# Two queues for the first loads, and the second layer's sums on VectorE

## The chip, the cores and the metric

One NeuronCore of one Trainium2 chip. The metric is the device time of one execution, in microseconds; of several executions the median is taken.

## What is computed

Three stages follow each other. The float64 inputs of the two layers' weights are read as pairs of words and turned into float32 on the chip.

```
# attention: 4 x 8 heads, 576 positions, 64 wide; window 128, slope per head
scores = where(mask, q @ k.T / 8 - slope * distance, -1e9)
attn   = softmax(scores);  x = attn @ v          # x: 2304 x 512
# layer 1: 512 -> 2048 -> 512, rational function
h = x @ w_in;  g = (a0 + a1 h + a2 h^2 + a3 h^3) / (1 + |b0||h| + |b1| h^2 + 1e-6)
x = g @ w_out
# layer 2: 512 -> 2048 -> 512, ELU
h = x @ w2_in; g = where(h > 0, h, exp(min(h, 0)) - 1)
out = g @ w2_out
```

## The kernel before

**Order of the work.** The program is written for manual scheduling: every engine runs its instructions in the order in which the Python code emits them, and an instruction at the head of an engine's queue that waits holds up all behind it. Tiles are named after the buffers in which they lie, so that `q_wi` is a tile of q in a slot that later holds a piece of `w_in`.

**Attention** runs over 16 units (a pair of heads of one batch element). `load(u, what)` (L336 to 356) brings q, k or v of a unit into SBUF by three DMAs, two of 128 KB and a tail of 32 KB, all issued by `nc.sync`, SP's queue (L348, L352). Ahead of the loop the loads of units 0 and 1 are issued in the order q0, k0, q1, k1, v0, v1 (L634 to 638). Those of unit u+2 are issued where unit u has been transposed. The hand-written list STEPS gives, for each turn t of the loop, the order of some 65 steps and the unit (t plus an offset) on which each works: `qT` and `kT` are TensorE's transposes of q and k (L418), with offsets 3 and 2, `qC` and `kC` their copies out of PSUM by ScalarE and VectorE (L441, L443), `zT` the tails' transposes (L432), S0 to S4 the score matmuls (L456, L474) and D0 to D8 VectorE's additions of the bias with a running extreme (L500). The transpose of q of unit 2 therefore stands in TensorE's order ahead of score matmuls of unit 1. Before all this, ScalarE's table of functions is loaded (L1255), and TensorE does warm-up matmuls on zeros (L646).

**Layer 1** goes over 6 blocks of 384 tokens and 16 pieces of 128 hidden features. Every product is made of three float32r passes (high x high, low x high, high x low): a value is split into a rounded high part, copied by ScalarE, and the rest, subtracted by VectorE or GpSimd.

**Layer 2** multiplies blocks by a scheme with seven products in place of eight. It goes over 3 blocks J of 768 tokens and 8 pairs p of hidden pieces, 24 steps q. A step has seven first products (`product`, L918) called b11, b21, t2, t3, t1, t4, b22, and four second ones (`gemm2`, L934). The factors t1 to t4 and s1 to s4 are sums:

- `sum_w(q)` (L837 to 848) makes the four sums of weights of a step, four operations of 128x256, into two tiles s; they are also written to DRAM (`keep_sums`) and read back for the later blocks (`load_sums`). So they are made for steps 0 to 7 alone.
- `sum_x(J, n)` (L881 to 896) makes one of the four sums of activations of a block, two operations of 128x384, in place of the block before it (which is used up by then) in xT.

Sums, and every other operand, are then split by `hi_w` (L870) or `hi_op` (L905) on ScalarE and `lo` (L875) on VectorE. A first product lies in one of two PSUM banks until VectorE has added it to what it belongs to (`added`, L974); ELU follows with two ScalarE operations (L980, L984), one on VectorE (L989) and the split of the result (L1006, L875).

The order of layer 2 is made by a planner, `in_order`: `step(key, engine, cost, fn, *needs)` notes each piece of work with a cost in ns, and what it needs. A due time is worked out backwards from the users. Then, always for the engine that can begin first, the ready step with the earliest start is taken, and of those within 60 ns the one with the earliest due time. A step on SP counts as done 3500 ns after its cost, any other 200 ns after. TensorE's own order is fixed. Products cost 1040 ns (first) and 2080 ns (second).

The lines that matter here: of the weight sums (L1051), step 0 is made ahead of the plan by VectorE (AT_DVE), w = 1 is planned on VectorE at 1400 ns, and w = 2 to 7 on GpSimd at 3500 ns. They need the load of the step's weights (`load_wi`, L810), the splits of step w-1's sums, since they use the same two tiles, and its `kept`. The activation sums (L1084) of block 0 are made by VectorE ahead of the plan, and those of blocks 1 and 2 are planned on GpSimd at 2300 ns each, sum n after product b11 of step 3+n, or 11+n, and after the splits of block J-1.

Of the kernel before, what the change touches and what calls it, by code (L numbers as in the profile page):

```python
# [44 lines left out]
def kernel(  # L45
# [13 lines left out]
    nc = tc.nc  # L59
# [40 lines left out]
    def place(key, shape, dtype, what):  # L100
        nm = "_".join(map(str, SLOT[key]))
        return wpool.tile(shape, dtype, tag=nm, name=f"{what}_{nm}")
# [107 lines left out]
    def cv_tile(shape, dtype, name, n=None):  # L210
        n = next(n_cv) if n is None else n
        return cv.tile(shape, dtype, tag=f"cv{n}", name=f"{name}{n}")
# [112 lines left out]
    def attention():  # L325
        with ExitStack() as es:
# [11 lines left out]
            def load(u, what):  # L338
                b, p = units[u]
                for nm in what:  # L340
                    src = {"q": q, "k": k, "v": v}[nm]
                    shape = [P, NF + 1, 2, D]
                    if nm == "v":
                        t = vt[u % 2]
                    else:
                        t = place(LATE["qk".index(nm) * 2 + u % 2], shape, F32, nm)
                    for e in range(2):
                        nc.sync.dma_start(  # L348
                            out=t[:, 0:NF, e, :],
                            in_=src[b, 2 * p + e, 0:NF * P, :].rearrange("(t p) d -> p t d", p=P),  # L350
                        )
                    nc.sync.dma_start(  # L352
                        out=t[0:TL, NF, :, :],
                        in_=src[b, 2 * p:2 * p + 2, NF * P:S, :].rearrange("h p d -> p h d"),
                    )
                    raw_t[nm, u] = t
# [254 lines left out]
            def run(step, u):  # L611
# [7 lines left out]
                elif 0 <= u < NU:  # L619
# [8 lines left out]
                    elif step == "Y":  # L628
                        if u + 2 < NU:
                            load(u + 2, "v")  # L630
                        else:
                            load_some(2)

            load(0, "q")  # L634
            load(0, "k")
            load(1, "qk")
            load(0, "v")
            load(1, "v")

            zero = place(order[19], [P, 4 * P], F32, "zero")  # L640
            nc.vector.memset(zero, 0.0)
# [51 lines left out]
    def experts():  # L693
# [47 lines left out]
        OPS, XO, sums, G, sq, kept, low_part = {}, {}, {}, {}, {}, {}, {}  # L741
# [65 lines left out]
        def load_wi(q):  # L807
            two[q] = t = at(q, "C", [P, 2, PC], F32, "two")
            for e in range(2):
                nc.sync.dma_start(out=t[:, e], in_=joined["wi", KF + q % NP2 * 2 + e])  # L810
# [26 lines left out]
        def sum_w(q, eng=nc.gpsimd, ns=range(4)):  # L837
            w = two[q]
            a11, a12, a21, a22 = [w[:, e, h * HC:(h + 1) * HC] for e in range(2) for h in range(2)]
            if 0 in ns:  # L840
                sq[q] = [cv_tile([P, 2, HC], F32, "s", n) for n in range(2)]
            s = sq[q]
            for n in ns:
                x, y, op = (
                    (a21, a22, ALU.add), (s[0][:, 0], a11, ALU.subtract), (a11, a21, ALU.subtract),
                    (a12, s[0][:, 1], ALU.subtract),
                )[n]
                eng.tensor_tensor(out=s[n // 2][:, n % 2], in0=x, in1=y, op=op)

        def keep_sums(w):  # L850
            kept[w] = [dram.tile([P, PC], F32, name=f"sums_{w}_{n}") for n in range(2)]
            for d, t in zip(kept[w], sq[w]):
                nc.sync.dma_start(out=d, in_=t.rearrange("p s c -> p (s c)"))
# [6 lines left out]
        def hi_w(q, x):  # L860
            if x in "CD":
                src = sq[q]["CD".index(x)].rearrange("p s c -> p (s c)")
            elif x == "B":
                src = two[q][:, 1, HC:PC]
            elif x == "A":
                src = two[q][:, 0]
            else:
                src = pair[0][:, "EF".index(x)]
            OPS[q, x] = t = at(q, x, [P, 2, HC if x == "B" else PC], F32R, "op")
            nc.scalar.activation(out=t[:, 0], in_=src, func=AF.Copy)  # L870
            low_part[q, x] = (t[:, 1], src, t[:, 0])

        def lo(key, eng=nc.vector):
            out, src, hi = low_part.pop(key)
            eng.tensor_tensor(out=out, in0=src, in1=hi.bitcast(F32), op=ALU.subtract)  # L875

        def x_row(J, k, T):
            c0 = (2 * J + T) * TB
            return xT[:, k, c0:c0 + TB]

        def sum_x(J, n, eng=nc.gpsimd, ks=range(2)):  # L881

            if 0 not in ks:
                pass
            elif J == 0:
                nm = "_".join(map(str, t_slots[n]))
                t = wpool.tile([P, 2, TB], F32, tag=nm, name=f"t_{nm}")
                sums[J, n] = [t[:, k] for k in range(2)]
            else:
                sums[J, n] = [x_row(J - 1, k + 2 * (n // 2), n % 2) for k in range(2)]  # L890
            for k in ks:
                b11, b21, b12, b22 = [x_row(J, k + 2 * i, T) for T in range(2) for i in range(2)]
                x, y = (
                    (b12, b11), (b22, sums[J, 0][k]), (b22, b12), (b21, sums[J, min(n, 1)][k]),
                )[n]
                eng.tensor_tensor(out=sums[J, n][k], in0=x, in1=y, op=ALU.subtract)
# [63 lines left out]
        def step(key, engine, cost, fn, *needs):  # L960
            todo[key] = (engine, cost, fn, needs)
            if engine == "PE":
                pe_order.append(key)
# [71 lines left out]
        def weight_steps(w):  # L1035

            def part(x, cost_hi, cost_lo, *needs):
                step((w, "hi", x), "ACT", cost_hi, lambda: hi_w(w, x), *needs)
                step((w, "lo", x), "DVE", cost_lo, lambda: lo((w, x)), (w, "hi", x))

            if w == 0:
                step((w, "kept"), "SP", 1200, lambda: keep_sums(w))
            else:
                out_gone = [(w - 2, "out", T, t) for T in range(2) for t in range(NTT)]
                if w > 1:
                    step((w, "load"), "SP", 1200, lambda: load_wi(w), (w - 3, "t1"), (w - 3, "t2"))
                gone = [(w - 1, "lo", "C"), (w - 1, "lo", "D")]
                if w >= NP2:
                    step((w, "sum"), "SP", 1200, lambda: load_sums(w), *gone)
                else:  # L1050
                    eng, cost, at = (nc.vector, 1400, "DVE") if w == 1 else (nc.gpsimd, 3500, "POOL")  # L1051
                    step((w, "sum"), at, cost, lambda: sum_w(w, eng), (w, "load"), *gone, (w - 1, "kept"))
                    step((w, "kept"), "SP", 1200, lambda: keep_sums(w), (w, "sum"))
                part("A", 520, 600, (w, "load"), (w - 3, "b11"), (w - 3, "b21"), *out_gone)
                part("B", 300, 340, (w, "load"), (w - 3, "t4"), *out_gone)
                part("C", 520, 600, (w, "sum"), (w, "lo", "A"), (w, "lo", "B"))
                part("D", 520, 600, (w, "sum"), (w - 3, "t3"), (w - 3, "b22"), *out_gone)
            for e, x in enumerate("EF"):
                gone = [(w - 2, "G", n) for n in ((0, 3), (1, 2))[e]]
                if e in raw_ones(w):  # L1060
                    if w > 0:
                        step((w, "raw", x), "SP", 600, lambda e=e: load_raw(w, e), *gone)
                    step((w, "scale", x), "ACT", 570, lambda e=e: scale_wo(w, e), (w, "raw", x), (w - 1, "lo", x),
                         (w - 1, "keep", x))
                    step((w, "words", x), "DVE", 1600, lambda e=e: join_wo(w, e), (w, "scale", x))
                    step((w, "keep", x), "SP", 600, lambda e=e: keep_wo(w, e), (w, "words", x))
                else:
                    step((w, "words", x), "SP", 600, lambda e=e: load_wo(w, e), (w - 1, "lo", x),
                         (w - 1, "keep", x), (w - NP2, "keep", x))
                part(x, 520, 600, (w, "words", x), *gone)  # L1070
# [9 lines left out]
        def x_sums(J, q):  # L1080

            used = [("xlo", J - 1, nm, k) for nm in ORDER for k in range(2)]
            for n in range(4):
                step(("sum", J, n), "POOL", 2300, lambda n=n: sum_x(J, n), *used, (q - 4 + n, "b11"),  # L1084
                     *[("sum", J, i) for i in range(n)])

        def second(q):
# [164 lines left out]
        last_pair()  # L1252

    with tc.manual_schedule():
        nc.scalar.preload_act_table_set("natural_log_exp_and_others")  # L1255
        attention()
        experts()

# [29 lines left out]
```

## Time and profile before

| | |
|---|---|
| median of 3 runs | 953.41 us (953.21 to 955.58) |
| profiled execution | 951.87 us, of which the span of the trace is 950.2 |
| TensorE, VectorE, ScalarE busy | 97%, 86%, 78% |
| GpSimd busy | 26% |
| chain that ended last | TensorE 63%, VectorE 18%, ScalarE 14%, issue 4%, DMA 1% |
| stages | attention to about 160 us, layer 1 to about 560, layer 2 to the end |

Busy times count an engine's instructions; for TensorE matmuls are pipelined, so what tells is the time in which it does nothing. A timeline row gives the start, the duration, engine, line, operation and tiles (out<-in) and, in brackets, how long the engine had been idle before it and what ended that. PEclk is the granted clock of TensorE as a share of its full 2.4 GHz. SPq is the issuing of DMAs by SP.

### The profile page before, as it was taken

Reading aid. Unit: us, or ns where it says so; the run is one execution under the profiler, and the core shown is the slowest. Engines: PE = TensorE matmul, PEld = TensorE weight load, DVE = VectorE, ACT = ScalarE, POOL = GpSimd, SP = SyncE. Lnnn points to the kernel's source line nnn. Section 1 sums busy time; section 2 is a strip of 40 time slices with the busy share of each in tenths; the row PEclk is TensorE's granted clock in tenths of the full one; section 3 lists DMA queues with packets and bytes.
Section 4 is the critical chain, followed back from the end, with each engine's and each line's share of the span. In section 5 each row is a group of like instructions: output and inputs, shape, how many; then the busy total and the mean of one; then the engine's idle time right before and its main releaser. Section 6 shows DMA issues by size and latency. Waiting matters only on the chain.

```text
span 950.2 us, 16856 instructions
## 1 busy us (share of the span) xinstructions
PE 920.9 (97%) x5494; PEld 839.0 (88%) x5494; DVE 818.8 (86%) x1890; ACT 745.1 (78%) x1635; POOL 248.6 (26%) x312
## 2 busy tenths in 40 slices
PE   7999998999999999999999999999999999999998
PEld 5766767999999999999999988878889898989897
DVE  5999998999999999999999999899987678787653
ACT  4999999889889889889888986656777566766553
POOL 4777772122222222222222225350310000000000
PEclk8999999999999999999999999999999999999999
DMA  6899943011231222222210034434344332443201
GB/s 165 207 236 242 235 135 95 1 34 34 84 100 51 84 83 68 84 67 86 82 46 28 26 120 125 142 122 152 104 140 149 100 100 68 162 141 96 78 1 67
DMA packets 112424, 98.36 MB, mean 104 GB/s; under 512 B 62800, under 2 KB 86096, under 8 KB 112336
## 3 DMA queue, kind: packets, MB, share of 16 engines
q1 hardware_dynamic: 112336, 97.29, 35.1%
q8 instruction: 43, 0.70, 0.3%
q14 instruction: 45, 0.37, 0.1%
HBM read 79.96 MB, written 17.30 MB: 102 GB/s over the span
## 4 chain that ended last, share of the span: by engine, by line
PE 63%; DVE 18%; ACT 14%; issue 4%; DMA 1%; POOL 0%; SPq 0%; DVEq 0%; ACTq 0%; POOLq 0%
PE acc L934 17%; PE h L260 15%; PE acc L705 15%; PE m L918 14%; ACT pT L441 2%; ACT pr_wo L515 2%; ACT pr_wi L515 2%; DVE ghi L301 2%; DVE qq L304 1%; DVE ee L322 1%; DVE ee L318 1%; DVE qq L313 1%; DVE h L321 1%; DVE op_wi L875 1%; DVE op_wo L875 1%
## 5 line engine op out<-in xcount | busy, mean ns | idle before, releaser
L260 PE MATMUL h<-xs,w_wi 128*128 128x384 f32 x1152 | 218.1, 335 | 1.3 <-ACT xs L235 0.8
L260 PEld LDWEIGHTS h<-xs,w_wi 128*128 128x128 f32 x1152 | 200.4, 188 | 4.2 <-DVE xs L236 2.4
L705 PE MATMUL acc<-ghi,w_wo 128*128 128x384 f32 x768 | 195.0, 334 | 0.0
L319 POOL TENSOR_TENSOR glo<-ee,rr 128x384 fp32r<-128x384 f32 x92 | 93.5, 1016 | 315.8 <-DVE ee L318 160.9
L705 PEld LDWEIGHTS acc<-ghi,w_wo 128*128 128x128 f32 x768 | 138.7, 188 | 0.0
L705 PE MATMUL acc<-glo,w_wo 128*128 128x384 f32 x384 | 128.7, 335 | 0.9 <-DVE glo L319 0.5
L934 PE MATMUL acc<-op_wo,ghi 128*128 128x512 f32 x288 | 89.6, 392 | 0.0
L307 ACT ACTIVATE rr<-qq,c_q 128x384 f32<-128x384 f32 x96 | 59.3, 618 | 38.5 <-DVE qq L304 37.7
L918 PE MATMUL m<-xo_wo,op_wi 128*128 128x384 f32 x336 | 77.1, 337 | 7.2 <-DVE ee L974 4.0
L918 PE MATMUL m<-xo_wi,op_wi 128*128 128x384 f32 x336 | 77.2, 337 | 0.0
L980 ACT ACTIVATE oo<-qq 128x384 f32<-128x384 f32 x24 | 12.6, 525 | 79.0 <-DVE qq L974 79.0
L705 PEld LDWEIGHTS acc<-glo,w_wo 128*128 128x128 f32 x384 | 72.1, 188 | 2.0 <-POOL glo L319 1.2
L918 PEld LDWEIGHTS m<-xo_wo,op_wi 128*128 128x128 f32 x336 | 60.4, 188 | 13.0 <-DVE qq L974 3.7
L290 ACT ACTIVATE oo<-h,a_sb 128x384 f32<-128x384 f32 x96 | 67.8, 706 | 4.6 <-DVE h L321 3.7
L293 ACT ACTIVATE ee<-h,a_sb 128x384 f32<-128x384 f32 x96 | 67.5, 703 | 0.0
L301 DVE TENSOR_TENSOR ghi<-ee,rr 128x384 fp32r<-128x384 f32 x96 | 53.6, 558 | 12.2 <-ACT oo L290 0.5
L322 DVE TENSOR_TENSOR ee<-ee,h 128x384 f32<-128x384 f32 x96 | 53.2, 555 | 10.0
L934 PEld LDWEIGHTS acc<-op_wo,ghi 128*128 128x128 f32 x288 | 53.5, 188 | 8.9
L918 PEld LDWEIGHTS m<-xo_wi,op_wi 128*128 128x128 f32 x336 | 60.5, 188 | 0.0
L304 DVE SCALAR_TENSOR_TENSOR qq<-h,b_abs,qa 128x384 f32<-128x384 f32 x92 | 55.9, 608 | 3.7 <-ACT qa L289 3.7
L974 DVE TENSOR_TENSOR ee<-ee,m 128x384 f32<-128x384 f32 x96 | 52.5, 547 | 5.2 <-PE m L918 5.1
L934 PE MATMUL acc<-op_wo,glo 128*128 128x512 f32 x144 | 57.0, 396 | 0.0
(203 smaller groups left out, 2175.1 us busy)
## 6 DMA issues: line engine op xcount, KB each, us to landing
pair<-joined_wo SPq DMA_DIRECT2D x43, 256.0 KB, 2.7
raw_wo<-in_moe_w_out_dram SPq DMA_DIRECT2D x20, 512.0 KB, 5.1
raw_wi<-in_moe_w_in_dram SPq DMA_DIRECT2D x16, 512.0 KB, 4.6
half<-in_moe_w_in_dram SPq DMA_DIRECT2D x32, 256.0 KB, 2.7
two_wo<-joined_wi SPq DMA_DIRECT2D x32, 256.0 KB, 2.9
s<-sums SPq DMA_DIRECT2D x32, 256.0 KB, 2.8
half<-in_moe_w_out_dram SPq DMA_DIRECT2D x22, 256.0 KB, 2.8
v<-in_v_dram SPq DMA_DIRECT2D x32, 128.0 KB, 3.2
```

Of the source, the lines that this page charges most:

```text
L260: nc.tensor.matmul(h, lhsT=WT["wi", f][:, SEL[wp], kk * P:(kk + 1) * P], rhs=x[xp][kk], start=(kk == 0 and n == 0), stop=(kk == KD - 1 and ...
L290: nc.scalar.activation(out=oo, in_=h2, func=AF.Identity, scale=a_sb[:, 3:4], bias=a_sb[:, 1:2])
L293: nc.scalar.activation(out=ee, in_=h2, func=AF.Identity, scale=a_sb[:, 2:3], bias=a_sb[:, 0:1])
L301: nc.vector.tensor_tensor(out=hi, in0=ee0, in1=rr0, op=ALU.mult)
L304: nc.vector.scalar_tensor_tensor(out=qq, in0=h2, scalar=b_abs[:, 1:2], in1=qa, op0=ALU.mult, op1=ALU.add)
L307: nc.scalar.activation(out=rr, in_=qq, func=AF.Ln, bias=c_q)
L319: (nc.gpsimd if c > 4 else nc.vector).tensor_tensor(out=low, in0=ee0, in1=rr0, op=ALU.mult)
L322: nc.vector.tensor_tensor(out=ee, in0=ee, in1=h, op=ALU.add)
L705: nc.tensor.matmul(acc_t[d], lhsT=WT["wo", f][:, SEL[wp], d * P:(d + 1) * P], rhs=gt[SEL[xp]], start=(f == 0 and n == 0), stop=(f == KF - ...
L918: nc.tensor.matmul(out, lhsT=w[:, SEL[wp], c0:c0 + P], rhs=XO[q // NP2, nm, k][:, SEL[xp]], start=(k == 0 and n == 0), stop=(k == 1 and n ...
L934: nc.tensor.matmul(acc_t[T, t], lhsT=gt[SEL[xp]][:, t * P:(t + 1) * P], rhs=w[:, SEL[wp]], start=(first and n == 0), stop=(last and n == 2),)
L974: nc.vector.tensor_tensor(out=t, in0=R[q, x], in1=M[q, m], op=ALU.add)
```

## The change

The loads of k of units 0 and 1 are issued by `nc.scalar`, ScalarE's queue. ScalarE's table load comes behind them in its queue: the call moves from the top of the program to behind the first loads. In the second layer all planned weight sums and activation sums go to VectorE, with planned costs of 1400 ns and 950 ns; the planner, with these costs and that engine, makes the order anew. Block 0's and step 0's sums were on VectorE already. The order of `load(0, "q")` and `load(0, "k")` stays as it was.

```
             def load(u, what):
                 b, p = units[u]
                 for nm in what:
+                    eng = nc.scalar if u < 2 and nm == "k" else nc.sync
...
                     for e in range(2):
-                        nc.sync.dma_start(
+                        eng.dma_start(
...
-                    nc.sync.dma_start(
+                    eng.dma_start(
...
-            load(0, "q")
-            load(0, "k")
+            load(0, "qk")
             load(1, "qk")
             load(0, "v")
             load(1, "v")
+            nc.scalar.preload_act_table_set("natural_log_exp_and_others")
...
-                    eng, cost, at = (nc.vector, 1400, "DVE") if w == 1 else (nc.gpsimd, 3500, "POOL")
-                    step((w, "sum"), at, cost, lambda: sum_w(w, eng), (w, "load"), *gone, (w - 1, "kept"))
+                    eng = nc.vector
+                    step((w, "sum"), "DVE", 1400, lambda: sum_w(w, eng), (w, "load"), *gone, (w - 1, "kept"))
...
             for n in range(4):
-                step(("sum", J, n), "POOL", 2300, lambda n=n: sum_x(J, n), *used, (q - 4 + n, "b11"),
+                step(("sum", J, n), "DVE", 950, lambda n=n: sum_x(J, n, nc.vector), *used, (q - 4 + n, "b11"),
...
     with tc.manual_schedule():
-        nc.scalar.preload_act_table_set("natural_log_exp_and_others")
         attention()
```

## Rows read from the trace of the kernel before

**Rows 1.** Page, busy us of each engine (share of the span), instructions.
```profile
PE 920.9 (97%) x5494; PEld 839.0 (88%) x5494; DVE 818.8 (86%) x1890; ACT 745.1 (78%) x1635; POOL 248.6 (26%) x312
```

**Rows 2.** Windows: length, busy us (instructions) per engine, PEclk, DMA share, GB/s.
```profile
560.00:665.00 105.00, 97.64 (x483) 86.19 (x482) 97.73 (x167) 67.88 (x137) 36.87 (x32) 1.00 0.42 134
665.00:700.00 35.00, 33.06 (x164) 29.25 (x163) 31.97 (x54) 24.72 (x52) 11.63 (x8) 1.00 0.35 106
700.00:800.00 100.00, 100.00 (x499) 89.96 (x497) 73.73 (x141) 65.90 (x135) 0.00 (x0) 1.00 0.38 120
```

**Rows 3.** Timeline of TensorE, 560 to 700: the four longest gaps.
```profile
567.66 0.77 PE L918 MATMUL m<-xo_wo,op_wi 128*128 128x384 f32 x3 [2.26 <-DVE ee L974]
...
593.90 0.79 PE L918 MATMUL m<-xo_wo,op_wo 128*128 128x384 f32 x3 [1.73 <-DVE ee L974]
...
642.36 0.79 PE L918 MATMUL m<-xo_wo,op_wi 128*128 128x384 f32 x3 [2.86 <-DVE qq L974]
...
683.56 0.79 PE L918 MATMUL m<-xo_wo,op_wi 128*128 128x384 f32 x3 [1.75 <-DVE ee L974]
```

**Rows 4.** Timeline of SP's queue at the start: q0, k0, and q2.
```profile
0.80 0.99 SPq L348 DMA_DIRECT2D q_wi<-in_q_dram  x2
...
2.60 1.14 SPq L348 DMA_DIRECT2D k_wi<-in_k_dram  x2
...
11.85 1.07 SPq L348 DMA_DIRECT2D q_wi<-in_q_dram  x2
```

**Rows 5.** Timeline of TensorE at the start: warm-up, and around its first gap.
```profile
1.52 3.78 PE L646 MATMUL warm<-zero_wo 128*128 128x512 f32 x4 [1.52 <-DVE zero_wo L641]
...
11.86 0.38 PE L474 MATMUL s_ps<-qkT 64*128 64x256 f32 x1
15.07 0.63 PE L418 MATMUL ps_qk<-ident,q_wi 128*128 128x128 f32 x4 [2.83 <-DMA q_wi<-in_q_dram]
```

**Rows 6.** Windows of the attention stage, columns as in rows 2.
```profile
4.00:12.00 8.00, 7.48 (x44) 4.70 (x42) 4.37 (x18) 2.95 (x9) 2.48 (x10) 1.00 0.72 164
18.00:22.00 4.00, 4.00 (x19) 2.83 (x19) 2.22 (x10) 2.59 (x12) 2.30 (x5) 0.50 0.73 168
16.00:30.00 14.00, 13.52 (x109) 10.20 (x108) 9.98 (x51) 12.17 (x44) 7.61 (x16) 0.76 0.70 172
40.00:130.00 90.00, 85.25 (x842) 62.92 (x844) 89.28 (x344) 90.00 (x283) 68.94 (x103) 1.00 0.88 217
```

**Rows 7.** Timeline of VectorE: its first operation behind TensorE's gap.
```profile
16.58 0.29 DVE L500 CUSTOM_DVE_ANT_0 pr_wi<-s_ps,bias_wo 128x128 f32<-128x128 f32 x1 [1.32 <-PE s_ps L474]
```

**Rows 8.** Timeline of ScalarE: its first two instructions.
```profile
0.80 1.28 ACT L1255 ACT_TABLE_LOAD   x1 [0.80 <-PEq L1272]
6.19 0.60 ACT L441 ACTIVATE qkT<-ps_qk 128x512 f32<-128x512 f32 x1 [4.11 <-PE ps_qk L418]
```

**Rows 9.** Timeline of VectorE: first of four sums of w = 1, and what follows.
```profile
563.16 0.42 DVE L848 TENSOR_TENSOR s<-two_wo 128x256 f32<-128x256 f32 x1
...
564.63 0.55 DVE L974 TENSOR_TENSOR qq<-ee,m 128x384 f32<-128x384 f32 x1
```

**Rows 10.** Groups by shape, VectorE, 700 to 800 us: count | busy us, mean ns.
```profile
L875 DVE TENSOR_TENSOR op_wo<-pair,op_wo 128x512 fp32r<-128x512 f32 x11 | 7.6, 687 | 1.6 <-ACT op_wo L870 1.6
...
L875 DVE TENSOR_TENSOR glo<-h,ghi 128x384 fp32r<-128x384 f32 x10 | 5.5, 551 | 0.0
```

**Rows 11.** Timeline of VectorE, 560 to 700: first, one, and last of 31.
```profile
571.19 1.09 DVE L989 SCALAR_TENSOR_TENSOR h<-h,ee 128x384 f32<-128x384 f32 x1
...
588.86 1.23 DVE L875 TENSOR_TENSOR op_wo<-pair,op_wo 128x512 fp32r<-128x512 f32 x1
...
692.02 1.50 DVE L875 TENSOR_TENSOR op_wo<-pair,op_wo 128x512 fp32r<-128x512 f32 x1
```

**Rows 12.** Timelines of SP and GpSimd: a load, and the sum that waits for it.
```profile
611.82 0.79 SPq L810 DMA_DIRECT2D two_wi<-joined_wi  x2
...
615.38 0.74 POOL L848 TENSOR_TENSOR s<-two_wi 128x256 f32<-128x256 f32 x1 [9.53 <-DMA two_wi<-joined_wi]
```

## The prediction

> **What bounds the kernel now.** I read the page's busy line first: over the span of 950.2 us TensorE is busy 97% and VectorE 86%, GpSimd 26% [rows 1]. A change that moves vector work and loads can only gain where TensorE stands still, so the next view is the table by windows of the second layer. From 700 us on TensorE is busy 100.00 us of 100 while VectorE has 26 us free: nothing done there shows in the time. From 560 to 700 it lacks (105.00 - 97.64) + (35.00 - 33.06) = 9.30 us, and VectorE is busy 97.73 of 105 and 31.97 of 35 us [rows 2]. The TensorE timeline puts 8.60 of these 9.30 us into four gaps (2.26, 1.73, 2.86, 1.75), each ended by a VectorE addition at L974 that empties a PSUM bank [rows 3]. So VectorE bounds that stretch. All 40 sums of the second layer on GpSimd (24 of weights at L848, 16 of activations at L896) lie in it: 32 + 8 instructions, 36.87 + 11.63 = 48.50 us of GpSimd, none later [rows 2].
>
> The other place is the start, in the timeline of SP's queue: it issues q, k of unit 0, q, k of unit 1, v, v, then q of unit 2, every load of three DMAs taking 1.8 us (0.80 to 2.60), so that q of unit 2 goes out at 11.85 [rows 4]. TensorE, whose order has this transpose next, waits 2.83 us for it, to 15.07 [rows 5]. Afterwards the granted clock is 0.50 (1.2 GHz) from 18 to 22, against 1.00 (2.4 GHz) before the gap [rows 6].
>
> **The start, step by step.** Six DMAs (k of units 0 and 1) leave SP: 6 x 0.6 = 3.6 us. Nothing else in SP's order changes, so v and then q and k of unit 2 go out 3.6 us earlier: 11.85 - 3.6 = 8.2. The transposes of unit 0 that read q's old buffer are over by then. Data 15.07 - 11.85 = 3.2 us after issue means 11.5, before TensorE is through with 11.86 + 0.38 = 12.24: the gap goes, 2.83 us for TensorE. The engines that carry the data were 72% busy at 164 GB/s while SP alone issued [rows 6], so there is room for about 164/0.72 = 228 GB/s; six loads of 288 KB plus q's 256 KB are 1.98 MB, 8.7 us at that rate, from some 2 us on: 10.7, still early enough. Two queues at once can make q of unit 0 a few tenths later; four warm-up matmuls occupy TensorE until 1.52 + 3.78 = 5.3 anyway [rows 5], so I cost that at nothing; uncovered, it is at most the 288 KB of k ahead of it, 1.3 us.
>
> How much of 2.83 reaches the end? VectorE stood idle 1.32 us just before its first operation behind the gap, at 16.58 [rows 7], and that goes: lower end 1.3. From 16 to 30 it is busy 9.98 of 14 [rows 6], so 4.02 idle, 0.58 of it before 16.58: upper end 1.32 + 3.44 = 4.8. TensorE alone could give more, 2.83 plus (1 - 0.76) x 14 = 3.4 for the lost clock, so the gain is what VectorE can follow. Its waits there are for score matmuls at the low clock, so I take a little over half of the 3.44: 1.3 + 2.0 = 3.3 us. From 40 to 130 ScalarE (90.00 of 90) and VectorE (89.28) are full [rows 6]; that stage starts earlier as a whole, its loads with it, and layer one hangs on its end, so the 3.3 us are kept.
>
> ScalarE now issues six DMAs, then the table load of 1.28 us. At SP's pace: 0.80 + 6 x 0.61 + 1.28 = 5.74, ahead of its first copy at 6.19 [rows 8]. Cost nothing, with 0.45 us of cover; no row shows ScalarE issuing a DMA, and at 0.8 us each the copy comes 0.7 late, with all behind it. The Trainium skill speaks against this edit: ScalarE: Activation LUTs, section What ACT_TABLE_LOAD costs, has a load followed by a drain of about 1.38 us, 2.66 in all. By that the copy would come at 7.1, an estimated 0.9 us late, and the start would pay 2.4 instead of 3.3. No trace here shows the drain: nothing stood behind the load until 6.19.
>
> **The sums, step by step.** On VectorE four sums of 128x256 take 564.63 - 563.16 = 1.47 us, as the step for w = 1 shows, which is on VectorE already [rows 9]. Six such steps: 8.8 us. A 128x384 operation with both inputs in SBUF takes 0.55 us [rows 10]; sixteen are 8.8 us, half for block 1 and half for block 2. GpSimd took 48.50 for all. But GpSimd's sums also stretch VectorE: 31 of its operations from 571.19 to 692.02 are lengthened, a 128x384 one to 1.09 and a 128x512 one to 1.23 or 1.50 [rows 11], where the same forms take 0.55 to 0.69 beside an idle GpSimd [rows 10]. Each against its own form's mean, the 31 add up to 18.2 us: 13.0 by 640 (23 of them), 5.2 from 672 on (8). Operations that read PSUM are not lengthened. All 18.2 us go when GpSimd falls silent.
>
> The sums of block 2 wait in the planner's order for product b11 of steps 11 to 14, which lies behind 700 where VectorE has 26 us free in 100: 4.4 us at no cost. Without that cover they would cost at most their 4.4. Into 560 to 665 go 8.8 + 4.4 = 13.2 us. The room there is 7.27 idle (105 - 97.73) plus 13.0 unstretched, less the 5.1 us by which the stretch gets shorter (1.73 + 2.86 and half a us of small gaps): 15.2. It fits, with VectorE 98% busy.
>
> Gap by gap: 2.26 at 567.66 lies before the first lengthened operation and stays. Of 1.73 at 593.90 the cause is four operations from 588.86 on, lengthened by 2.13 together: it goes. Ahead of 642.36 five operations are lengthened by 3.6 against 2.86: it goes. Ahead of 683.56 it is 4.0 against 1.75, and block 2's sums are gone: it goes. With the 0.70 of small ones that is 7.04 at most. What is late next are the additions behind a sum: ten blocks of 0.9 to 1.5 us now stand in VectorE's queue, and TensorE has about 3.1 us (a second product and a first one, 2080 and 1040 ns in the planner) between a product and the next that needs its sum. I reckon two of the ten cost 1 us each: 5.0, between 0 and 7.0. Nothing is behind GpSimd any more.
>
> **Sum.** 3.3 + 5.0 = 8.3. The profiled execution took 951.87 (span 950.2 and 1.67 around it): 943.6 by its own time. The median of the runs is 1.54 above it; against that, 953.41 - 8.3 = 945.1, say 945.
>
> **The rivals.** *Start pays nothing.* Issuing from two queues need not halve the issue time: if the 0.6 us per DMA are spent in something both queues share, q of unit 2 goes out at 11.85 as before. Then only the sums pay: 948.4. For it: the engines moving data were never full at the start, so something ahead of them sets 0.6. Against it: SP's issues follow each other without a gap, like work of SP itself. The skill's page DMA: Bandwidth & Descriptors, section Queues, rings and completion order, says that neither queue has a descriptor generator of its own, which is this case; its section Issuing engines are not separate DMA queues grants that a second engine saves issue time, which is the forecast. No run here shows which.
>
> *Sums pay nothing.* VectorE at 98% keeps it the bound; the gaps return under other names. Only the start pays: 950.1. For it: 2.0 us of room in 100. Against it: weight steps run one step ahead of need, and 13.2 of work takes the place of 13.0 of stretching.
>
> *Neither*: 953.
>
> *Slower: VectorE stands behind a load.* A sum waits for its weights and for the sums' buffers; on GpSimd that stopped nobody (9.53 us at 615.38), in VectorE's queue every addition behind it stops. Issue to sum took 615.38 - 611.82 = 3.56 us [rows 12]; the planner allows 1200 + 3500 ns = 4.7, so VectorE stands only if SP is over 1.1 us late. At 2 us for each of six steps it is 12 us, all of it in the end since VectorE is full: 945.1 + 12 = 957. It is slower from 8.3/6 = 1.4 us a step on.
>
> **How the numbers follow.** Forecast 0.60; only the sums 0.13; only the start 0.15, half of it better than 950.5; neither 0.06; slower 0.06. A measurement of this kernel tells about 0.3% (2.9 us) from no change. Faster by more: 0.60 + 0.13 + 0.07 = 0.80; within: 0.08 + 0.06 = 0.14; slower 0.06. The range runs from both parts near their upper ends (4.8 + 7.0 = 11.8 would be 941.6; as the clock can give more, 940.5) to the start alone at a bit under its middle, 951.
>
> **What would show it.** Right: TensorE's transposes of unit 2 begin near 12.3 with no wait for q; clock 1.00 from 16 to 24; ScalarE's first copy still near 6.2; no GpSimd after 560; no VectorE operation of 128x512 above 0.75 us after 560; TensorE's gaps from 560 to 700 about 4 us, the one of 2.26 among them. Wrong: VectorE idle ended by a DMA ahead of L848; ScalarE's copy at 7; the same 9 us of gaps.

## The result and the profile after

The changed kernel took 940.61 us (median; 940.24 to 943.22) against 953.31 us (952.39 to 955.58) on the same chip: a ratio of 0.9872, 95% interval 0.9857 to 0.9887, or 12.7 us less. The forecast of 945.0 had the sign, the two parts and the place of each right, and was 4.4 us too high. The profiled execution took 940.24 us with a span of 938.2, so 12.0 us of span went, and the two traces say where.

The first fence is the page's busy line of the changed kernel, in the columns of [rows 1].

```profile
PE 916.1 (98%) x5494; PEld 837.2 (89%) x5494; DVE 815.4 (87%) x1930; ACT 747.6 (80%) x1635; POOL 199.9 (21%) x272
```

VectorE has 40 instructions more than in [rows 1] and is busy 3.4 us *less*. Four weight sums take 1.47 us up to the next operation [rows 9] and two activation sums 0.94 (605.69 to 606.63 in VectorE's timeline), so the forty add 6 x 1.47 + 8 x 0.94 = 16.3 us, and some 20 us of lengthening went with GpSimd's operations; the prediction had 18.2. GpSimd's 48.7 us less are the 48.50 of [rows 2].

Next the windows of the changed kernel, columns as in [rows 2]: the attention stage first, then the second layer, which now begins 2.86 us earlier. The DMA share adds up the times of all packets over 16 engines, so it can pass 1.

```profile
4.00:12.00 8.00, 6.09 (x35) 3.12 (x34) 3.47 (x15) 3.30 (x7) 2.48 (x10) 1.00 1.08 188
16.00:30.00 14.00, 12.93 (x123) 10.13 (x124) 12.70 (x61) 13.39 (x47) 10.87 (x21) 1.00 0.80 222
540.00:650.00 110.00, 107.68 (x554) 98.78 (x553) 105.47 (x218) 82.08 (x164) 5.09 (x5) 1.00 0.41 142
650.00:690.00 40.00, 40.00 (x199) 35.85 (x198) 35.06 (x71) 28.53 (x60) 0.00 (x0) 1.00 0.38 132
690.00:790.00 100.00, 100.00 (x499) 90.06 (x498) 77.63 (x151) 66.30 (x135) 0.00 (x0) 1.00 0.33 111
```

From 16 to 30 the granted clock is 1.00 (2.4 GHz) where it was 0.76, and VectorE gets 12.70 us of work done where it had 9.98 [rows 6]. From 540 to 650 TensorE lacks 2.32 us, and from 650 nothing. In TensorE's timeline those 2.32 are nearly all one gap, the second line here; the first is the transpose of unit 2 that waited 2.83 us in [rows 5].

```profile
13.11 0.66 PE L420 MATMUL ps_qk<-ident,q_wi 128*128 128x128 f32 x4
...
564.82 0.77 PE L920 MATMUL m<-xo_wo,op_wi 128*128 128x384 f32 x3 [2.23 <-DVE ee L976]
```

No wait stands in brackets behind the transpose: it starts when TensorE gets to it, 1.96 us earlier than before. The gap of 2.23 is the first one of [rows 3], the one forecast to stay. The other three are gone.

The whole gain splits at the first product of the second layer, here in TensorE's timeline of the kernel before and of the changed one:

```profile
551.37 0.68 PE L918 MATMUL m<-xo_wo,op_wo 128*128 128x384 f32 x3
548.51 0.68 PE L920 MATMUL m<-xo_wo,op_wo 128*128 128x384 f32 x3
```

In this pair of executions **2.86 us come from the start**. From there to the end of TensorE's last matmul it is 395.09 us before and 385.96 after: **9.13 us come from the sums**. Together 11.99 of the 12.0.

Groups by shape, VectorE, 545 to 700 us, first of the changed kernel (count | busy us, mean ns of one):

```profile
L877 DVE TENSOR_TENSOR op_wo<-pair,op_wo 128x512 fp32r<-128x512 f32 x18 | 12.4, 688 | 0.0
L877 DVE TENSOR_TENSOR glo<-h,ghi 128x384 fp32r<-128x384 f32 x15 | 8.3, 554 | 0.0
L850 DVE TENSOR_TENSOR s<-two_wo 128x256 f32<-128x256 f32 x10 | 4.2, 419 | 0.0
L898 DVE TENSOR_TENSOR xT<-xT 128x384 f32<-128x384 f32 x8 | 4.1, 556 | 0.0
```

and the first two of these groups in the kernel before, same stretch and columns:

```profile
L875 DVE TENSOR_TENSOR op_wo<-pair,op_wo 128x512 fp32r<-128x512 f32 x16 | 14.5, 909 | 0.0
...
L875 DVE TENSOR_TENSOR glo<-h,ghi 128x384 fp32r<-128x384 f32 x13 | 9.1, 703 | 0.1
```

Their means fall from 909 to 688 ns and from 703 to 554, the figures of [rows 10]. The sums of weights (L850) and of activations (L898) have no idle time before them: no sum waits for a load, which was the slower rival's mechanism. Only 8 sums of L898 lie here; those of block 2 run from 724.00 to 772.14, where VectorE has room.

The start, in the timeline of SP's queue (q of unit 0, v of unit 0, q of unit 2),

```profile
0.80 0.98 SPq L350 DMA_DIRECT2D q_wi<-in_q_dram  x2
...
5.74 0.93 SPq L350 DMA_DIRECT2D v<-in_v_dram  x2
...
9.45 1.07 SPq L350 DMA_DIRECT2D q_wi<-in_q_dram  x2
```

and of ScalarE with its queue:

```profile
0.80 1.09 ACTq L350 DMA_DIRECT2D k_wi<-in_k_dram  x2
1.92 0.69 ACTq L354 DMA_DIRECT2D k_wi<-in_k_dram  x1
2.64 1.68 ACTq L350 DMA_DIRECT2D k_wo<-in_k_dram  x2
5.22 0.61 ACTq L354 DMA_DIRECT2D k_wo<-in_k_dram  x1
5.86 1.28 ACT L640 ACT_TABLE_LOAD   x1 [5.86 <-DMA k_wi<-in_k_dram]
7.16 0.60 ACT L443 ACTIVATE qkT<-ps_qk 128x512 f32<-128x512 f32 x1
```

ScalarE's first load goes out at the pace of SP, the second does not: six issues end at 5.83, where 0.80 + 6 x 0.61 = 4.46 was forecast. The table load then ends at 7.14, and the first copy comes at 7.16 in place of 6.19 [rows 8]. SP is slowed as well: q of unit 2 goes out at 9.45, not 8.2 as forecast nor 11.85 as in [rows 4]. It is slow only while ScalarE issues too. Its first six DMAs take from 0.80 to 5.74; the six of v, alone, take from 5.74 to 9.45, or 0.62 each, which is its pace of [rows 4]. The windows of these two stretches (columns as in [rows 2]) show the engines that carry the data fuller in the second:

```profile
0.80:5.80 5.00, 4.22 (x9) 1.87 (x10) 1.51 (x4) 0.00 (x0) 4.66 (x15) 1.00 0.91 177
5.80:9.45 3.65, 1.81 (x10) 0.82 (x9) 1.24 (x3) 1.88 (x2) 0.75 (x6) 1.00 1.24 194
```

### The profile page after: what moved, and what is told of

It reads as the page before. It is cut to its first block, busy times and chain, and to the rows that moved or that the text cites. A ratio compares the mean times of both kernels' runs of the same rounds, so it can differ in the third digit from the quotient of the medians.

```text
span 938.2 us, 16811 instructions
## 1 busy us (share of the span) xinstructions
PE 916.1 (98%) x5494; PEld 837.2 (89%) x5494; DVE 815.4 (87%) x1930; ACT 747.6 (80%) x1635; POOL 199.9 (21%) x272
## 4 chain that ended last, share of the span: by engine, by line
PE 70%; ACT 13%; DVE 13%; issue 2%; DMA 1%; SPq 0%; DVEq 0%; ACTq 0%
PE acc L936 21%; PE m L920 18%; PE h L260 14%; PE acc L707 14%; ACT pT L443 2%; ACT pr_wi L517 2%; DVE ghi L301 2%; ACT pr_wo L517 2%; DVE ee L322 2%; DVE qq L304 2%; DVE ee L318 1%; DVE qq L313 1%; DVE h L321 1%; ACT cvt L134 1%; PE s_ps L476 1%
```

## The experiments

**One part alone.** Two theories on the gain: the parts are independent and add, or the earlier start only changes when the second layer's waits happen. Each kernel takes one part of the change back:

```diff
# start_only: the sums as before
-                    eng = nc.vector
-                    step((w, "sum"), "DVE", 1400, lambda: sum_w(w, eng), (w, "load"), *gone, (w - 1, "kept"))
+                    eng, cost, at = (nc.vector, 1400, "DVE") if w == 1 else (nc.gpsimd, 3500, "POOL")
+                    step((w, "sum"), at, cost, lambda: sum_w(w, eng), (w, "load"), *gone, (w - 1, "kept"))
-                step(("sum", J, n), "DVE", 950, lambda n=n: sum_x(J, n, nc.vector), *used, (q - 4 + n, "b11"),
+                step(("sum", J, n), "POOL", 2300, lambda n=n: sum_x(J, n), *used, (q - 4 + n, "b11"),
# sums_only: the loads as before
-                    eng = nc.scalar if u < 2 and nm == "k" else nc.sync
...
-                        eng.dma_start(
+                        nc.sync.dma_start(
...
-                    eng.dma_start(
+                    nc.sync.dma_start(
...
-            load(0, "qk")
+            load(0, "q")
+            load(0, "k")
```

(sums_only also puts the table load back at the kernel's first place.)

> Only the first loads and the table load are moved; the second layer's sums are planned and made as before. The changed kernel's trace has unit 15's tail product 2.9 us earlier than before and ScalarE's first copy at 7.16 instead of 6.19. If the two parts are independent: 953.3 - 2.9 = 950.4. If the earlier start is lost again before the second layer ends (the layer's gaps take it): 953.

> Only the sums go to VectorE; first loads as before. If the parts are independent: 953.3 - 9.1 = 944.2, with the 2.83 us gap at 15.07 and one gap of about 2.2 us left in the second layer. If my step for the sums was right in size (5.0): 948.3.

Measured: start_only 951.03 us (948.84 to 952.03; ratio 0.9983, 0.9973 to 0.9994), sums_only 942.72 (942.61 to 943.18; 0.9902, 0.9882 to 0.9921). Against before (952.67 beside them) that is 1.6 and 9.9 us; the first lies near the 950.4 of independent parts, the second 1.5 us below its 944.2. The interval of start_only, 0.6 to 2.6 us, does not reach 2.86, while on top of the sums the start is worth 0.9902 - 0.9872 of the time, or 2.9 us.

The traces tell why. start_only has its first second-layer product at 548.56, sums_only takes 385.96 us from that product to the end, the changed kernel's own figures within 0.05. (Five kernels with the new start have this product at 548.35 to 549.30, w_only below at 550.76; the start of before has it at 551.37 and 550.88.) But start_only's layer takes 398.03, 2.94 *more* than before. Its TensorE timeline has the gaps of [rows 3] unchanged:

```profile
639.58 1.33 PE L920 MATMUL m<-xo_wo,op_wi 128*128 128x384 f32 x3 [2.85 <-DVE qq L976]
...
682.17 0.79 PE L920 MATMUL m<-xo_wo,op_wi 128*128 128x384 f32 x3 [1.76 <-DVE ee L976]
```

and its windows (columns as in [rows 2]) tell what is new:

```profile
636.00:644.00 8.00, 5.15 (x20) 4.37 (x19) 7.79 (x13) 3.67 (x7) 1.79 (x2) 0.79 0.33 110
680.00:688.00 8.00, 6.24 (x24) 5.11 (x23) 8.00 (x18) 5.40 (x12) 0.46 (x1) 0.79 0.22 66
```

A mean granted clock of 0.79: part of each window ran at 0.50 (1.2 GHz), at the gap or within 1.5 us behind it, and behind the first gap three products took 1.33 us in place of 0.79 in [rows 3]. Set beside the shift of the same matmuls before, these two falls cost 1.4 and 1.5 us. In the profiled execution of before the same gaps have no fall. So the gaps of the second layer carry a risk beside their length, and start_only paid it in its profile; seven of its ten runs show the profile's mean clock of 0.996, and the two fastest, 948.84 and 949.53, show 0.999. What a start alone is worth (1.6 by the medians, 2.81 by its first product) depends on it.

**Engine or order?** Naming VectorE changes two things: who executes the sums, and how the planner orders all that stands beside them, since it is told another engine and another cost. Two kernels cross them.

```diff
# dve_plan_pool: the order of the changed kernel, GpSimd executes
-                    eng = nc.vector
+                    eng = nc.vector if w == 1 else nc.gpsimd
-                step(("sum", J, n), "DVE", 950, lambda n=n: sum_x(J, n, nc.vector), *used, (q - 4 + n, "b11"),
+                step(("sum", J, n), "DVE", 950, lambda n=n: sum_x(J, n), *used, (q - 4 + n, "b11"),
# pool_plan_dve: the order of before, VectorE executes
-                    step((w, "sum"), "DVE", 1400, lambda: sum_w(w, eng), (w, "load"), *gone, (w - 1, "kept"))
+                    cost, at = (1400, "DVE") if w == 1 else (3500, "POOL")
+                    step((w, "sum"), at, cost, lambda: sum_w(w, eng), (w, "load"), *gone, (w - 1, "kept"))
-                step(("sum", J, n), "DVE", 950, lambda n=n: sum_x(J, n, nc.vector), *used, (q - 4 + n, "b11"),
+                step(("sum", J, n), "POOL", 2300, lambda n=n: sum_x(J, n, nc.vector), *used, (q - 4 + n, "b11"),
```

> The changed kernel's plan (costs and engine of the sums as VectorE's, so its order of emission), but the moved sums are executed by GpSimd. Theory 1, the sums on GpSimd stretch VectorE's work: gaps come back, 946 to 951. Rival, the gain is the planner's new order: 941.

> The plan of before (sums planned on GpSimd at 3500 and 2300 ns, so its order of emission), but executed by VectorE; first loads as in the changed kernel. Theory 1: no operation is stretched, 940.5 to 944. Rival, the gain is the new order: 948 to 951.

Measured: dve_plan_pool 948.66 us (946.02 to 950.86; ratio 0.9960, 0.9946 to 0.9973), pool_plan_dve 943.84 (943.32 to 944.61; 0.9913, 0.9896 to 0.9929). TensorE's longest gaps of the second layer, with GpSimd executing,

```profile
565.59 1.02 PE L920 MATMUL m<-xo_wo,op_wi 128*128 128x384 f32 x3 [2.25 <-DVE ee L976]
...
638.89 0.79 PE L920 MATMUL m<-xo_wo,op_wi 128*128 128x384 f32 x3 [2.98 <-DVE qq L976]
...
680.11 0.79 PE L920 MATMUL m<-xo_wo,op_wi 128*128 128x384 f32 x3 [1.75 <-DVE ee L976]
```

and with VectorE executing in the order of before:

```profile
564.80 0.76 PE L920 MATMUL m<-xo_wo,op_wi 128*128 128x384 f32 x3 [2.23 <-DVE ee L976]
...
635.76 0.79 PE L920 MATMUL m<-xo_wo,op_wi 128*128 128x384 f32 x3 [0.44 <-DVE qq L976]
...
655.48 0.79 PE L920 MATMUL m<-xo_wo,op_wi 128*128 128x384 f32 x3 [0.60 <-DVE ee L976]
```

The gap of 1.73 in [rows 3] goes with the new order alone; those near 640 and 680 keep their full size in either order as long as GpSimd executes. With VectorE executing they shrink to 0.44 and 0.60. The layer takes 393.72 us in the first and 389.76 in the second; without the clock fall of 1.5 that each has behind the gap near 565, 392.2 and 388.2. With 395.09 and 385.96 at the corners, the engine is worth 6.9 in the order of before and 6.2 in the new one, the order 2.9 and 2.3. Both count; the engine counts more than twice as much. Sums on GpSimd could also cost by being late themselves. In the kernel before they did not: from 551 to 700 the trace puts no wait of TensorE or VectorE down to GpSimd, and one of ScalarE, 1.1 us. In dve_plan_pool ScalarE waits 5.2 us for them, so lateness may have a part in the 6.2.

**Which sums?** One kind goes back to GpSimd, in engine and order.

```diff
# w_only: the activation sums back
-                step(("sum", J, n), "DVE", 950, lambda n=n: sum_x(J, n, nc.vector), *used, (q - 4 + n, "b11"),
+                step(("sum", J, n), "POOL", 2300, lambda n=n: sum_x(J, n), *used, (q - 4 + n, "b11"),
# x_only: the weight sums of steps 2 to 7 back
-                    eng = nc.vector
-                    step((w, "sum"), "DVE", 1400, lambda: sum_w(w, eng), (w, "load"), *gone, (w - 1, "kept"))
+                    eng, cost, at = (nc.vector, 1400, "DVE") if w == 1 else (nc.gpsimd, 3500, "POOL")
+                    step((w, "sum"), at, cost, lambda: sum_w(w, eng), (w, "load"), *gone, (w - 1, "kept"))
```

> The changed kernel with the activation sums (16 operations of 128x384) planned and made by GpSimd again; the weight sums stay on VectorE. Theory 1: the stretching that lay beside the activation sums comes back, and with it the gaps near 642 and 683: 5 to 6 us above the changed kernel, 945 to 947, up to 3 more if the clock falls behind the gaps. Rival, only the weight sums' place in the plan matters: 941.

> The changed kernel with the weight sums of steps 2 to 7 planned and made by GpSimd again; the activation sums stay on VectorE. Theory 1: the gap near 594 comes back (2.0) with the small ones: 2 to 4 us above the changed kernel, 942.5 to 944.5. Rival: 949 to 950, all of the second layer's gain lost.

Measured: x_only 942.32 us (942.17 to 943.44; ratio 0.9892, 0.9877 to 0.9908), close to what was expected: its layer takes 388.20 us, 2.24 more than the changed kernel's. w_only 951.55 (950.84 to 954.04; 0.9989, 0.9977 to 1.0) is above the 945 to 947 expected and above the 950 that allowed for the clock. In its trace the layer takes 396.16 us, 10.2 more than in the changed kernel: with 16 operations on GpSimd instead of 40 the gain of the sums is gone. (Its start is 2.2 us late too, with a clock of 0.79 from 8 to 16, though it is the changed kernel's start.) TensorE's timeline of w_only has one gap that no other kernel has,

```profile
572.99 1.30 PE L920 MATMUL m<-xo_wo,op_wi 128*128 128x384 f32 x3 [8.14 <-DVE ee L976]
```

and GpSimd's timeline shows the cause:

```profile
559.27 10.16 POOL L898 TENSOR_TENSOR xT<-xT 128x384 f32<-128x384 f32 x8
```

All eight sums of block 1 run at once, from 559.27 on. In the kernel before they come later and in smaller groups, since weight sums that wait for loads stand ahead of them in GpSimd's queue. GpSimd's timeline of before, a waiting weight sum and the first two activation sums:

```profile
598.78 1.01 POOL L848 TENSOR_TENSOR s<-two_wo 128x256 f32<-128x256 f32 x1 [5.82 <-DMA two_wo<-joined_wi]
...
603.23 2.62 POOL L896 TENSOR_TENSOR xT<-xT 128x384 f32<-128x384 f32 x2
```

In w_only nothing stands ahead, and they meet a stretch where VectorE has no room. VectorE's timeline of w_only:

```profile
559.66 1.37 DVE L877 TENSOR_TENSOR xo_wi<-t_wi,xo_wi 128x384 fp32r<-128x384 f32 x1
560.96 0.54 DVE L976 TENSOR_TENSOR ee<-ee,m 128x384 f32<-128x384 f32 x1
...
563.55 1.50 DVE L877 TENSOR_TENSOR op_wi<-two_wo,op_wi 128x512 fp32r<-128x512 f32 x1
...
566.23 1.21 DVE L850 TENSOR_TENSOR s<-two_wo 128x256 f32<-128x256 f32 x1
```

A 128x384 operation with both inputs in SBUF takes 1.37 us, a 128x256 one 1.21 where it took 0.42; the one between them, which reads PSUM (m), keeps its 0.54. The changed kernel's VectorE runs the same operations there in the same order: from the layer's first product to the addition that ends the gap it takes 15.62 us (548.51 to 564.13), w_only 21.54 (550.76 to 572.30). These 5.9 us are what the gap grew by, and the clock fell at it (0.72 from 568 to 580), another 1.5. So 7.4 of the 10.2 us hang on the place that one kind of sum gave the other in GpSimd's queue, and the price of a GpSimd operation is set by what VectorE has to do beside it. x_only agrees: its weight sums stand apart in time, and beside the gap that the changed kernel has too only the one near 594 came back.

```profile
564.70 0.76 PE L920 MATMUL m<-xo_wo,op_wi 128*128 128x384 f32 x3 [2.27 <-DVE ee L976]
...
590.92 0.79 PE L920 MATMUL m<-xo_wo,op_wo 128*128 128x384 f32 x3 [1.75 <-DVE ee L976]
```

**Does the late copy at the start cost anything?** table_first keeps the change and puts the table load ahead of ScalarE's issues.

```diff
-            nc.scalar.preload_act_table_set("natural_log_exp_and_others")
...
     with tc.manual_schedule():
+        nc.scalar.preload_act_table_set("natural_log_exp_and_others")
         attention()
```

> The changed kernel with ScalarE's table load ahead of its six DMA issues again. If the DMA issues, 5.0 us in the changed kernel instead of the 3.7 of my step, are what makes the first copy 0.97 late, the copy stays near 7.1 and the time at 940.6. If it is the table load's place, or a drain behind it: copy at 6.2, 939.7.

Measured: 941.17 us (939.26 to 942.14; ratio 0.9874, 0.9858 to 0.9890), not to be told from the changed kernel. ScalarE's timeline:

```profile
0.80 1.28 ACT L1256 ACT_TABLE_LOAD   x1 [0.80 <-PEq L1273]
...
5.18 0.65 ACTq L354 DMA_DIRECT2D k_wo<-in_k_dram  x1
6.19 0.60 ACT L443 ACTIVATE qkT<-ps_qk 128x512 f32<-128x512 f32 x1 [4.11 <-PE ps_qk L420]
```

The table load runs beside the issues (the first goes out at 0.83) and the copy is back at 6.19, 0.97 us earlier. Yet the first second-layer product is at 548.81, no earlier than 548.51. At TensorE's transposes of unit 2 the lead is down to 0.57 us (12.54, after 13.11 in the changed kernel), and it is gone by the end of this window (columns as in [rows 2]):

```profile
16.00:24.00 8.00, 7.70 (x48) 5.68 (x50) 7.04 (x37) 7.02 (x24) 5.21 (x11) 0.79 0.88 239
```

The clock fell, which it did not in the changed kernel's profile. One of the four runs kept a mean clock of 1.00; its span is 937.2 us, against 938.2 to 938.6 in the three such runs of the changed kernel. So without a fall the earlier copy may be worth about its 0.97 us; one run without a trace does not show it.

**A cheaper start?** What q of unit 2 needs is to stand earlier in SP's queue. Three kernels, all with the table load first and the sums on VectorE, get it by other means: v_late issues the v loads of units 0 and 1 behind q and k of unit 3; v_spread issues one there and the other behind q and k of unit 4; v_scalar sends these v loads, not k, through ScalarE's queue. The edits of v_late and v_spread are to the loads of the kernel before, that of v_scalar to the changed kernel's.

```diff
# v_late: all loads on SP
                             load(u + 2, "qk")
+                            if u == 1:
+                                load(0, "v")
+                                load(1, "v")
...
-            load(0, "v")
-            load(1, "v")
# v_spread: the same, but
+                            if u in (1, 2):
+                                load(u - 1, "v")
# v_scalar
-                    eng = nc.scalar if u < 2 and nm == "k" else nc.sync
+                    eng = nc.scalar if u < 2 and nm == "v" else nc.sync
```

> Sums as in the changed kernel; no load on ScalarE's queue, instead the first two loads of v are issued by SP behind q and k of units 2 and 3. q of unit 2 goes out at 8.1 without a second queue; first copy at 6.19, so the start pays about 3.9 instead of 2.9: 939.7. Rival, the two queues are what makes it faster: 943.

> All sums on VectorE; q and k of units 0 and 1 stay in SP's queue, v of units 0 and 1 go through ScalarE's instead, behind the table load. Theory (what counts is when SP issues q of unit 2, and that ScalarE's first copy is not late): SP's q of unit 2 at about 8.2 as in v_late, nothing added to SP's queue afterwards, so no wait for q of unit 4; ScalarE's first copy near 6.2 to 6.6; first second-layer product 0.5 to 1 us ahead of the changed kernel's 548.5, time 939.6 to 940.2. Rival (loads at the start share the engines that carry them, so v beside q and k delays q and k of units 0 and 1 by as much as the early copy gives): first copy at 7 or later, first product at 548.5 or later, time 940.6 to 941.5.

> As v_late (all loads on SP, sums on VectorE), but v of unit 0 goes out behind q and k of unit 3 and v of unit 1 behind q and k of unit 4. Theory (SP's issue time is one budget, and v_late spent it ahead of q of unit 4): q of unit 4 goes out 1.8 us earlier than in v_late, about 19.8, the wait of 2.8 us for it shrinks to 1 or less, and the time is 940 to 941.5. Rival (TensorE's wait moves on to v of unit 1 or q of unit 5, since the six DMAs are only moved): one wait of 2 us or more is left between 24 and 40, the first second-layer product stays near 551, and the time is 942.5 to 943.5.

Measured: v_late 943.01 us (942.65 to 946.59; ratio 0.9902, 0.9885 to 0.9919), v_scalar 942.51 (940.77 to 943.68; 0.9874, 0.9857 to 0.9890), v_spread 944.03 (942.95 to 944.50; 0.9894, 0.9879 to 0.9908). None beats the changed kernel (v_scalar's ratio is not to be told from its own), and all three theories missed; each time the rival is nearer, v_late's 943 to the digit. In v_late q of unit 2 does go out at 8.16 and is in time. In its SP queue the v loads then push q of unit 4 to 21.56, after 18.68 in the changed kernel,

```profile
15.71 1.15 SPq L348 DMA_DIRECT2D v<-in_v_dram  x2
...
21.56 0.93 SPq L348 DMA_DIRECT2D q_wi<-in_q_dram  x2
```

and TensorE waits there instead:

```profile
27.00 1.09 PE L418 MATMUL ps_qk<-ident,q_wi 128*128 128x128 f32 x4 [2.83 <-DMA q_wi<-in_q_dram]
```

v_spread brings q of unit 4 forward to 18.86 and cuts that wait to 1.23; the transposes behind it start 0.33 us after the changed kernel's (25.10). The larger loss comes with the next unit: q of unit 5 goes out at 28.45, after 25.50 in the changed kernel, and another gap follows, with a clock of 0.79 from 32 to 40 (SP's queue, then TensorE's timeline):

```profile
28.45 0.93 SPq L348 DMA_DIRECT2D q_wo<-in_q_dram  x2
...
25.43 0.63 PE L418 MATMUL ps_qk<-ident,q_wi 128*128 128x128 f32 x4 [1.23 <-DMA q_wi<-in_q_dram]
...
34.78 0.63 PE L418 MATMUL ps_qk<-ident,q_wo 128*128 128x128 f32 x4 [1.67 <-DVE qq L527]
```

The view puts this gap down to VectorE, one of whose operations ends at that very moment. But the trace has the second DMA of this q landing at 34.65. In the waits for q of 2.83 ([rows 5] and v_late) and of 1.23, TensorE starts 0.13 to 0.14 us after that landing, and so it does here. It is a wait for a load again, as the rival said.

In v_scalar the loads of k and q that TensorE needs first come late, as its rival said:

```profile
8.67 0.27 PE L434 MATMUL ty<-ident,k_wi 64*128 64x64 f32 x1 [0.65 <-DMA k_wi<-in_k_dram]
...
9.89 1.09 PE L420 MATMUL ps_qk<-ident,q_wo 128*128 128x128 f32 x4 [0.95 <-DMA q_wo<-in_q_dram]
```

The first second-layer product is at 551.30 in v_late, 551.17 in v_spread and 551.75 in v_scalar, no better than 550.88 in sums_only, which changes nothing at the start, although the first copy is early in all three (6.19, 5.58 and 6.26). v_scalar's profile is of one of its longer executions (span 941.5 us, clock 0.79 from 8 to 16 and from 16 to 24), so it says less than the other two; its run with a mean clock of 1.00 has a span of 938.7, level with the changed kernel's. The reading that fits v_late and v_spread: q of unit 2 is one of a row of loads that SP issues only just in time, so what is put ahead of a later q in SP's queue makes that unit wait, while the change takes six issues out of the queue. v_scalar takes six out as well; without a clock fall it is not shown to be slower than the change.

## Why the prediction came out as it did

*The place and the mechanism of the sums: right.* VectorE operations go back to the durations of [rows 10], the gap of 2.26 stays as 2.23, the other three go, block 2's sums run beside room, and nobody waits for a load.

*The size of the sums term: wrong.* It said 5.0: 7.04 of gaps, less 2.0 because "two of the ten cost 1 us each" of the blocks of sums ahead of additions. Two things failed in it. The deduction of 2.0: TensorE's idle time from the first product on went from 9.37 to 2.32 us, so all 7.05 of the gaps went and none of the ten blocks made a new one. pool_plan_dve says in part why: with VectorE executing in the order of before, 3.42 us stay idle, so 1.1 of the 2.0 came there. The planner's new order, to which the prediction gave no term, takes that away too and is worth 2.3 to 2.9 in all. And the equation of a gap with its idle time: the layer got 9.13 shorter for 7.05 of idle time, 2.08 more over the seven gaps that went (nine before, two after), 0.3 each. About 0.1 of it is seen, as three products take 0.77 to 0.79 behind a gap [rows 3] and 0.68 elsewhere; since the ends of matmuls are modelled, the rest can't be placed. The measured 9.13 lies outside the 0 to 7.0 that the prediction gave as its ends. Of the 4.4 us by which the forecast was too high, this term makes 4.1. That 940.61 still lies inside 940.5 to 951, by 0.1, is luck: the lower end was built from 7.0 for the sums, 4.8 for the start and 1.1 for the clock, and the sums passed theirs while the start stayed 1.9 below its own.

*The start: right in mechanism, 0.4 too high in the traces.* 3.3 was forecast and 2.86 came in this pair of executions, 1.6 by the medians of start_only. The wait of 2.83 went, the clock stayed at 1.00 from 16 to 24, and VectorE followed. Two steps on the way were off. Two queues at once are not two queues at full pace: 18 DMAs were out by 9.45 us (12 from SP, 6 from ScalarE) where SP alone had needed until 11.85, so 2.4 us were won of the 3.6 forecast. Full engines by themselves do not explain it: SP was back at 0.62 us per DMA from 5.74 on, with the engines at a share of 1.24, and slow before, at 0.91, while both queues issued. What the two queues share no run here shows. Nor did the rate reach the 228 GB/s that the prediction reckoned with: from 4 to 12 it is 188, at a share of 1.08. The transposes of unit 2 began at 13.11, not near 12.3, because the work ahead of them was itself late. And ScalarE's copy came 0.97 us late, which was one of the marks of "wrong". The Trainium skill, page ScalarE: Activation LUTs, section What ACT_TABLE_LOAD costs, would have it at 7.1 by a drain behind the load; it came at 7.16, but no drain is in the trace: the load ends at 5.86 + 1.28 = 7.14 and the copy starts 0.02 later. What made it late is the six issues ahead of the load.

*The rivals.* "Start pays nothing" falls with the 2.81 us of start_only's first product, though its mechanism was there in part: by 5.83 us the two queues had issued 12 DMAs, where SP alone at 0.61 us issues 8. The Trainium skill's DMA: Bandwidth & Descriptors, section Queues, rings and completion order, which stood behind it, is borne out only in that issues from two queues slowed each other. "Sums pay nothing" falls with sums_only, "neither" with the result, and "slower" with the sums, none of which waits for a load.

*Against the medians.* The spans give 12.0, the medians 12.7. Before's median is 1.4 above its profiled execution, the changed kernel's 0.4 above its own. Clock falls have a part in this: three of the changed kernel's four runs show a mean clock of 1.000, and the runs of before taken beside the experiments show 0.991 to 0.997. How large that part is, is not shown.

## What to carry to other kernels

Before moving small operations off a busy VectorE to an idle GpSimd, add up what they lengthen on VectorE: here 48.5 us of GpSimd's work cost about 20 us of VectorE's, more than the 16.3 that the same sums take on VectorE itself. And the place counts as much as the amount, so ask what a queue does once the operations ahead of the ones you left there are gone: sixteen unmoved sums, and a clock fall behind the gap that they made, took back all that moving twenty-four had won. Of a load that comes late, look first for a second queue for what is needed soonest; a reordering on the same queue only picked the unit that waits here.

## What was not expected of the hardware

*A TensorE gap can cost twice.* At the same gap of 2.2 to 2.3 us near 565 the mean granted clock from 564 to 572 stayed at 1.00 in seven kernels, before and the changed one among them, and was 0.79 in table_first, pool_plan_dve, dve_plan_pool and v_spread; the falls cost 1.5 to 1.6 us each. Behind gaps of 2.85 and 1.76 it fell in start_only and not in before. What decides it the runs don't show.

*The lengthening by GpSimd can more than double a VectorE operation.* Beside eight sums in a row 0.42 became 1.21, 0.55 became 1.37 and 0.69 became 1.50 when both inputs lay in SBUF; an addition with an input in PSUM stayed at 0.54. The Trainium skill, SBUF — State Buffer, section Who interferes with whom, has it that a VectorE instruction with two SBUF inputs contends with a GpSimd instruction that reads SBUF, and that one with at most one SBUF input, outside the two-port modes, does not; these rows agree, and give the size. One operation with a single SBUF input was lengthened too: in the kernel before, the shift of words at L137 (128x512) took 1.25 us at 638.48, beside two sums, and 0.41 to 0.42 elsewhere from 560 to 700; no run here shows in which mode it runs.

*A table load and DMA issues of the same engine overlap when the load stands first.* In table_first it runs from 0.80 to 2.08 with issues from 0.83 on; behind six issues, in the changed kernel, it starts only when the last of them is out.
